# Batch 0's last 64 tokens in 64x64 tiles over two banks, and the last score ahead of the token tail

## The chip, the cores and the metric

The kernel runs on one core of a Trainium2 chip. A core has TensorE (PE, matmuls; PEld is its weight loads), VectorE (DVE), ScalarE (ACT), GpSimd (POOL) and SyncE (SP, which here issues DMAs). They run beside each other and wait for each other through semaphores. TensorE writes its results to PSUM, here eight banks of 128 x 512 fp32, which VectorE and ScalarE read. The metric is the device time of the whole kernel in microseconds (us), as the median of several runs.

## The reference

For 8 batches, 12 heads, 448 tokens and 64 features a head:

```python
scores = q @ k.T / sqrt(64) - log(448)
attn   = sigmoid(scores)                       # no softmax
x      = attn @ v                              # heads side by side: (8, 448, 768)
h      = relu(x.T @ w_tok1) @ w_tok2           # mixes tokens: 448 -> 256 -> 448
u      = x + h.T
out    = u + relu(u @ w_ch1) @ w_ch2           # mixes channels: 768 -> 1536 -> 768
```

The kernel computes in fp16 with fp32 sums.

## The kernel before

Work goes in 24 cycles, three (`u` = 0, 1, 2) to each batch `b`; a cycle handles four heads. All order is written out by hand: each engine runs its instructions in the order in which the program records them, and the framework adds only the waits.

In a cycle, seven calls of `qk` (line 184) make the scores of 64 keys each against all queries: four 64x64 matmuls of 448 columns, one in each quarter of the array, into a two-bank buffer with the tag "qk", of which there are two. ScalarE's sigmoid (line 191) empties the buffer, so score j needs the sigmoid of score j-2. `av` (line 215) sums over the values for the cycle before; `tok_tail` (line 274) and `tok1` (line 293) are the first token matmul of an earlier cycle: the tail has only the last 64 tokens and runs in four 64x64 tiles, the other six matmuls are 128x128; ReLU follows on ScalarE (line 307). `ytrans` (line 316) is the second token matmul.

Between these, output groups of an earlier batch are computed: `ch2` (lines 549, 560 and 572 or 579) for 128 tokens by 384 outputs, and other forms of the same. Batch 0 differs from the later ones: the residual u is not added by VectorE from a transposed copy (`un`), but by three identity matmuls on TensorE, so VectorE only copies (line 579). The last 64 of the 448 tokens are a group of their own. `ch2_last` (lines 802, 813, 825) does it with 24 matmuls in 128x64 tiles (128 contraction rows, 64 tokens), two next to each other for the two halves of the outputs, in one bank; with the residual that is 6 matmuls more. For batches 1 to 6 `last_split` does it in 64x64 tiles instead: the contraction rows 0 to 63 and 64 to 127 go to different banks, `ps[0]` and `ps[1]`, four matmuls in a step (line 631), and VectorE adds the two.

At the end of a batch's third cycle `utrans` and `token_sums` (lines 330 and 442) prepare the next stage, and `sevens` (line 499) does the first channel matmul as seven block products; its first one takes a "qk" buffer.

Besides the two "qk" buffers there are four single banks, m0 to m3; `at_bank` says which is handed out next. Banks 0 and 1 serve the attention and token work, 2 and 3 the channel work.

The cycles c = 6, 7 and 8 (counted from 0; c = 8 has u = 2) spread a list `pending` of batch 0's output pieces over three calls of `work(share)` a cycle. `work` flips between banks 2 and 3 with each group, and after each piece takes one step from `copies` (relayouts of the next batch on VectorE, line 126, and the DMA transposes that follow them). In the cycle c = 8, `work(1)` ends the last full-width group, which is in bank 2; `work(2)` and `work(3)` are the group of the last 64 tokens, in bank 3. From c = 9 a second loop runs to c = 23; here `ch2_pair`, `last_split` and `ch2_split` (lines 375, 631) lie between the scores.

Of the kernel before, what the change touches and what calls it, by code (L numbers as in the profile page):

```python
# [10 lines left out]
FP32 = mybir.dt.float32  # L11
ADD = mybir.AluOpType.add
# [11 lines left out]
NU = 3  # L24
# [6 lines left out]
def kernel(  # L31
# [11 lines left out]
    nc = tc.nc  # L43
# [6 lines left out]
    NCB = CC // 128  # L50
    N_CYCLES = NU * B
    N_FIRST = 4
    DH = D // 2
# [10 lines left out]
    ident = pc.tile([128, 128], FP16, name="ident")  # L64
# [14 lines left out]
    uts = [pc.tile([128, NDB, 512], FP16, name=f"ut{n}") for n in range(2)]  # L79
# [5 lines left out]
    def bank(shape, dtype, name):  # L85

        if opening_banks:
            n = opening_banks.pop(0)
        else:
            n = at_bank[0]  # L90
            at_bank[0] = (n + 1) % 4
        return pp.tile(shape, dtype, tag=f"m{n}", bufs=1, name=name)
# [86 lines left out]
    def qk(b, u, j):  # L179
        att[b, u, j] = pa.tile([128, 2, S], FP16, tag="att", bufs=10, name=f"att_{b}_{u}_{j}")  # L180
        ps = pp.tile([128, 2, 512], FP32, tag="qk", bufs=2, name=f"qk_{b}_{u}_{j}")
        for g in range(2):
            for hi in range(2):
                nc.tensor.matmul(  # L184
                    out=ps[64 * g : 64 * g + 64, hi, 0:S],
                    lhsT=tr[b, "k"][64 * hi : 64 * hi + 64, u, j, 64 * g : 64 * g + 64],
                    rhs=tr[b, "q"][64 * hi : 64 * hi + 64, u, :, 64 * g : 64 * g + 64],
                    start=True,
                    stop=True,
                )  # L190
        nc.scalar.activation(  # L191
            out=att[b, u, j][:, :, :],
            in_=ps[:, :, 0:S],
            func=SIGMOID,
            bias=bias_t[:, :],
            scale=att_scale,
        )
# [427 lines left out]
    def split_steps(ps, n_cb, lhsT, rhs):  # L625

        def step(n):
            for r in range(2):
                part = slice(64 * r, 64 * r + 64)
                for m in (0, 64):  # L630
                    nc.tensor.matmul(  # L631
                        out=ps[r][m : m + 64, 0:DH],
                        lhsT=lhsT(part, n, m),
                        rhs=rhs(part, n, m),
                        start=(n == 0),
                        stop=(n == n_cb - 1),
                    )

        return [lambda n=n: step(n) for n in range(n_cb)]
# [21 lines left out]
    def last_split(b, ps):  # L661

        def end():
            o = pa.tile([128, DH], FP32, tag="outl", bufs=1, name=f"o_{b}_3")
            parts = [slice(0, 64), slice(64, 128)]
            nc.vector.tensor_tensor(
                out=o[:, :].rearrange("s (u d) -> s u d", d=128),
                in0=un[b][:, 0:NU, 3, :],
                in1=ps[0][:, 0:DH].rearrange("s (u d) -> s u d", d=128),
                op=ADD,  # L670
            )
            nc.vector.tensor_tensor(out=o[:, :], in0=o[:, :], in1=ps[1][:, 0:DH], op=ADD)
            for g in range(2):
                nc.sync.dma_start(
                    out=orow[b, NJ - 1][:, DH * g : DH * g + DH], in_=o[parts[g], :]
                )

        return split_steps(
            ps,
            NCB,  # L680
            lambda part, n, m: h2[b][part, BY_GROUP[n], 384:448],
            lambda part, n, m: c2[part, BY_GROUP[n], DH * (m // 64) : DH * (m // 64) + DH],
        ), end

    LOW, HIGH = slice(0, NCB // 2), slice(NCB // 2, NCB)
    D1, D2 = slice(0, DH), slice(DH, D)
# [234 lines left out]
    def pieces_ch2(b, groups):  # L921
        for t, half in groups:
            for n in range(0, NCB, 3):
                yield 3 * DH, lambda t=t, half=half, n=n: ch2(b, t, half, n, n + 3)

    def pieces_last(b):
        for n in range(0, NCB, 3):
            yield 3 * DH, lambda n=n: ch2_last(b, n, n + 3)
# [197 lines left out]
    def some(n):  # L1126
        for f in copies[:n]:
            f()
        del copies[:n]
# [3 lines left out]
    for c in range(2 * NU, ONE_RUN):  # L1133
        b, u = divmod(c, NU)
        before, ahead = divmod(c - 1, NU), divmod(c - 2, NU)


        if c == 2 * NU:
            first = c
            pending, shares = [*pieces_ch2(0, by_half[2:]), *pieces_last(0)], [10, 10, 10]  # L1140
            total = sum(w for w, f in pending)
            spent = 0

        def work(share):
            goal = 3 * sum(shares[: c - first]) + share * shares[c - first]
            done = 0
            while pending and spent + done < total * goal / 90:
                w, f = pending.pop(0)
                if len(pending) % 4 == 3:
                    lane[0] ^= 1  # L1150
                at_bank[0] = 2 + lane[0]
                f()
                done += w
                if copies:
                    copies.pop(0)()
                elif early:
                    early.pop(0)()
            return done

        some(len(copies))  # L1160
        qk(b, u, 0)
        qk(b, u, 1)
        at_bank[0] = 0
        av(*before)
        xtrans_dma(*before)
        qk(b, u, 2)
        if c == 2 * NU + 2:
            copies += through_dma(3, 0)[NU + 1 :]
        spent += work(1)
        qk(b, u, 3)  # L1170
        qk(b, u, 4)
        if u < 2:
            at_bank[0] = 0
            tok_tail(*ahead)
            tok1(*ahead, with_scores=True)
        spent += work(2)
        if c == 2 * NU + 2:
            utrans(b - 1)
            token_sums(b - 1)
            spent += work(3)  # L1180
        qk(b, u, 5)
        qk(b, u, 6)
        at_bank[0] = 0
        if u < 2:
            ytrans(*ahead)
        else:
            tok_tail(*ahead)
            tok1(*ahead, with_scores=True)
        if c == 2 * NU + 1:
            copies += through_dma(3, 0)[: NU + 1]  # L1190
        if u < 2:
            spent += work(3)
        if u == 2:
            sevens(b - 1)
            at_bank[0] = 0
            ytrans(*ahead)
            gated_loads(b)
    assert not copies and not pending and not early

    for c in range(ONE_RUN, N_CYCLES):  # L1200
        b, u = divmod(c, NU)
        before, ahead = divmod(c - 1, NU), divmod(c - 2, NU)
        if b == NU:
            within, behind = ((0, 0), (3, 3), (2, 0))[u]
        else:
            within, behind = ((0, 2), (2, 4), (0, 0))[u] if b < B - 1 else (2, 2)
        if u == 0:
            assert not copies
            copies += through_dma(b + 1, 0) if b + 1 < B else output_sums()

        X, Y = 2, 0
        at_bank[0] = X
        if u == 1:
            ps = [bank([128, 512], FP32, f"c2_{b - 2}_3_{r}") for r in range(2)]
            turn0, last_end = last_split(b - 2, ps)
            qk(b, u, 0)
            qk(b, u, 1)
            for f in turn0:  # L1220
                f()
            last_end()
            qk(b, u, 2)
        else:
            turn0, turn1, rest = ch2_pair(b - 2, u)
            part = len(turn1) * 2 // 3
            qk(b, u, 0)
            qk(b, u, 1)
            for f in turn0:
                f()  # L1230
            qk(b, u, 2)
            some(within)
            if c == ONE_RUN + 2:
                gated_loads(b)
        at_bank[0] = Y
        av(*before, 0, 4)
        qk(b, u, 3)
        av(*before, 4, NJ)
        xtrans_dma(*before)
        if u == 2:  # L1240
            utrans(b - 1)
            token_sums(b - 1)
        qk(b, u, 4)
        if u == 1:
            at_bank[0] = X
            turn1, rest = ch2_split(b - 2, u, 0)
            part = NCB // 2
        for f in turn1[:part]:
            f()
        qk(b, u, 5)  # L1250
        for f in turn1[part:]:
            f()
        if u == 1:
            rest()
            some(within)
        at_bank[0] = Y
        tok_tail(*ahead)
        qk(b, u, 6)
        tok1(*ahead, with_scores=True)
        if u == 1:  # L1260
            at_bank[0] = X
            ch2(b - 2, u, 1)
        else:
            rest()
        if u == 2:
            sevens(b - 1)
        at_bank[0] = Y
        ytrans(*ahead)
        some(behind)
        if u == 1 and NU < b < B - 1:  # L1270
            gated_loads(b)
# [93 lines left out]
```

## Time and profile before

| | |
|---|---|
| median of 3 runs | 344.91 us (344.31 to 345.24) |
| the profiled execution | 343.85 us, of which the span of the instructions is 341.9 |
| granted TensorE clock | 1.000 |
| TensorE busy | 334.7 us (98%) |
| VectorE, ScalarE busy | 216.7 us (63%), 212.5 us (62%) |
| chain that ended last | TensorE 90%, ScalarE 5%, the rest 1% each or less |

In the profile "L184" is line 184 of the kernel. A row of a timeline gives start, length, engine, line, operation, output<-inputs, tile and shape, and how many instructions it holds; in brackets the idle time before it and what ended it. The lengths of matmuls include their way through the array, so matmuls that follow each other overlap in it: what one costs is the time from its start to the next start.

### The profile page before, as it was taken

Reading aid. Unit: us, or ns where it says so; the run is one execution under the profiler, and the core shown is the slowest. Engines: PE = TensorE matmul, PEld = TensorE weight load, DVE = VectorE, ACT = ScalarE, POOL = GpSimd, SP = SyncE. Lnnn points to the kernel's source line nnn. Section 1 sums busy time; section 2 is a strip of 40 time slices with the busy share of each in tenths; the row PEclk is TensorE's granted clock in tenths of the full one; section 3 lists DMA queues with packets and bytes.
Section 4 is the critical chain, followed back from the end, with each engine's and each line's share of the span. In section 5 each row is a group of like instructions: output and inputs, shape, how many; then the busy total and the mean of one; then the engine's idle time right before and its main releaser. Section 6 shows DMA issues by size and latency. Waiting matters only on the chain.

```text
span 341.9 us, 10439 instructions
## 1 busy us (share of the span) xinstructions
PE 334.7 (98%) x4549; PEld 238.8 (70%) x4549; DVE 216.7 (63%) x438; ACT 212.5 (62%) x271; POOL 56.6 (17%) x98
## 2 busy tenths in 40 slices
PE   7999999999999999999999999999999999999994
PEld 4655566555886679766886679766896669768952
DVE  3376467588674775566574584666765685886662
ACT  4996846588658684877648785777648885102400
POOL 8992440040040004000130004000100000000000
PEclk9999999999999999999999999999999999999999
DMA  7999999999999799999999599948991438035406
GB/s 125 172 180 191 207 204 200 169 175 223 219 172 208 119 175 175 209 168 134 191 188 167 123 196 184 223 98 149 199 157 33 102 78 141 5 69 130 86 0 161
DMA packets 104380, 52.17 MB, mean 153 GB/s; under 512 B 76432, under 2 KB 101264, under 8 KB 104336
## 3 DMA queue, kind: packets, MB, share of 16 engines
q1 hardware_dynamic: 78944, 29.70, 47.8%
q0 software_dynamic: 25168, 21.50, 41.7%
q8 instruction: 35, 0.57, 0.7%
q10 hardware_dynamic: 224, 0.33, 0.3%
q14 instruction: 9, 0.07, 0.1%
HBM read 43.45 MB, written 11.01 MB: 159 GB/s over the span
## 4 chain that ended last, share of the span: by engine, by line
PE 90%; ACT 5%; DMA 1%; DVE 1%; issue 1%; ACTq 0%; DVEq 0%
PE c_ab L499 14%; PE qk L184 10%; PE c L549 9%; PE c_c L499 8%; PE c L375 8%; PE xa L215 8%; PE c L631 6%; PE tk L293 5%; PE yt L316 5%; ACT att L191 5%; PE c L763 4%; PE c L613 4%; PE c L352 3%; DMA first_q<-in_q_dram 1%; PE c L802 1%; PE c_a L499 1%
## 5 line engine op out<-in xcount | busy, mean ns | idle before, releaser
L191 ACT ACTIVATE att<-qk,att_bias 128x896 f16<-128x896 f32 x168 | 157.0, 1015 | 41.5 <-PE qk L184 41.1
L184 PE MATMUL qk<-tr_q,tr_k 64*64 64x448 f16 x672 | 57.5, 356 | 0.5 <-DVE tr_k L176 0.2
L499 PEld LDWEIGHTS <-c 128*128 128x128 f16 x504 | 48.4, 98 | 1.1 <-issue 0.3
L224 DVE CAST xT<-xa 128x448 f16<-128x448 f32 x46 | 26.6, 620 | 29.8 <-PE xa L215 29.8
L215 PE MATMUL xa<-att,raw_v 64*64 64x448 f16 x644 | 38.0, 349 | 0.0
L499 PEld LDWEIGHTS <-sum 128*128 128x128 f16 x378 | 36.3, 98 | 0.0
L184 PEld LDWEIGHTS <-tr_k 64*64 64x64 f16 x672 | 20.3, 105 | 19.7 <-issue 12.0
L572 DVE TENSOR_TENSOR o<-un,c 128x384 f32<-128x384 f16 x34 | 18.8, 554 | 23.3 <-PE c L613 10.2
L549 PE MATMUL c<-c,h 128*128 128x384 f16 x180 | 32.9, 326 | 0.0
L375 PE MATMUL c<-c,h 64*64 64x384 f16 x640 | 31.1, 322 | 0.0
L520 ACT ACTIVATE pt_ab<-c_ab 128x896 f32<-128x896 f32 x21 | 19.3, 917 | 16.9 <-PE c_ab L499 16.3
L323 DVE TENSOR_TENSOR ut<-xT,yt 128x448 f16<-128x448 f16 x48 | 27.5, 614 | 1.9 <-PE yt L316 1.9
L215 PEld LDWEIGHTS <-raw_v 64*64 64x64 f16 x672 | 20.3, 107 | 10.9 <-issue 0.4
L1039 POOL COPY gate<-tr_q 128x2 f16<-128x2 f16 x6 | 1.2, 195 | 154.0 <-DMA tr_q<-rel_q 154.0
L549 PEld LDWEIGHTS <-h 128*128 128x128 f16 x180 | 17.2, 98 | 11.3 <-issue 1.0
L307 ACT ACTIVATE h<-tk 128x256 f16<-128x256 f32 x42 | 14.2, 405 | 16.7 <-PE tk L293 16.7
L375 PEld LDWEIGHTS <-h 64*64 64x64 f16 x640 | 18.7, 107 | 7.9
L316 PE MATMUL yt<-w,h 128*128 128x448 f16 x96 | 22.1, 353 | 0.0
L631 PE MATMUL c<-c,h 64*64 64x384 f16 x480 | 22.1, 322 | 0.0
L522 ACT ACTIVATE h<-c_ab 128x896 f16<-128x896 f32 x7 | 6.4, 917 | 24.4 <-PE c_ab L499 24.4
L293 PE MATMUL tk<-xn,w 128*128 128x256 f16 x156 | 21.2, 274 | 0.1
L529 DVE TENSOR_TENSOR h<-pt_ab,c_ab 128x896 f16<-128x896 f32 x14 | 15.2, 1084 | 9.4 <-PE c_ab L499 9.4
(110 smaller groups left out, 473.3 us busy)
## 6 DMA issues: line engine op xcount, KB each, us to landing
out_dram<-o SPq DMA_DIRECT2D x48, 192.0 KB, 3.5
c<-in_moe_w_ch_dram POOLq DMA_DIRECT2D x4, 1152.0 KB, 15.6
raw_k<-in_k_dram POOLq DMA_DIRECT2D x10, 336.0 KB, 9.3
raw_q<-in_q_dram POOLq DMA_DIRECT2D x10, 336.0 KB, 13.3
raw_v<-in_v_dram POOLq DMA_DIRECT2D x10, 336.0 KB, 10.8
out_dram<-o SPq DMA_DIRECT2D x15, 96.0 KB, 2.2
raw_q<-in_q_dram POOLq DMA_DIRECT2D x12, 112.0 KB, 4.9
raw_k<-in_k_dram POOLq DMA_DIRECT2D x12, 112.0 KB, 4.8
```

The source lines that it names most:

```text
L184: nc.tensor.matmul(out=ps[64 * g : 64 * g + 64, hi, 0:S], lhsT=tr[b, "k"][64 * hi : 64 * hi + 64, u, j, 64 * g : 64 * g + 64], rhs=tr[b, " ...
L191: nc.scalar.activation(out=att[b, u, j][:, :, :], in_=ps[:, :, 0:S], func=SIGMOID, bias=bias_t[:, :], scale=att_scale,)
L215: nc.tensor.matmul(out=ps[g][64 * hi : 64 * hi + 64, 0:S], lhsT=raw[b, "v"][64 * g : 64 * g + 64, u, hi, j, :], rhs=att[b, u, j][64 * g : ...
L224: nc.vector.tensor_copy(out=xTs[b % 2][:, u, g, 0:S], in_=ps[g][:, 0:S])
L293: nc.tensor.matmul(out=ps[tcb], lhsT=w1[rows, t, cols], rhs=xn[b, u][rows, :, t, :], start=(t == 0 and not with_scores), stop=(t == (2 if ...
L316: nc.tensor.matmul(out=ps[:, 0:S], lhsT=h1[b, u][:, tcb, g, :], rhs=w2[:, tcb, :, :], start=(tcb == 0), stop=(tcb == 1),)
L323: nc.vector.tensor_tensor(out=uts[b % 2][:, db, 0:S], in0=xTs[b % 2][:, u, g, 0:S], in1=ps[:, 0:S], op=ADD)
L375: nc.tensor.matmul(out=ps[p][m : m + 64, 0:n], lhsT=lhsT(p, part, m), rhs=rhs(p, part), start=(first and turn == 0), stop=(last and turn = ...
L499: nc.tensor.matmul(out=ps[:, g, p, :], lhsT=weights[n][:, d, 128 * cb : 128 * cb + 128], rhs=moving[n][:, d, :], start=(n in (1, 5, 2) and ...
L520: nc.scalar.activation(out=shaped(part[:, :, :]), in_=ps, func=COPYF)
L549: nc.tensor.matmul(out=ps[:, 0:DH], lhsT=h2[b][:, BY_GROUP[cb], 128 * t : 128 * t + 128], rhs=c2[:, BY_GROUP[cb], cols], start=(cb == 0), ...
L631: nc.tensor.matmul(out=ps[r][m : m + 64, 0:DH], lhsT=lhsT(part, n, m), rhs=rhs(part, n, m), start=(n == 0), stop=(n == n_cb - 1),)
```

## The change

It has two parts.

In the cycle c = 8 the last-64-token group of batch 0 leaves `pending` and is done by `last_split`: twelve steps of four 64x64 matmuls and three steps of four 64x64 matmuls with 128 columns for the residual, over banks 2 and 3. `utrans` and `token_sums` are recorded ahead of it, eight steps come before score 5, which stood behind the whole group, and the rest stands between scores 5 and 6. VectorE then copies one bank and adds the other (128x384 each) where it made two copies of 64x384. The goals of `work` stay as they were, since `total` keeps the group's weight.

In the cycles c = 9 to 23, `qk(b, u, 6)` is recorded ahead of `tok_tail` instead of behind it.

```diff
@@ last_split
         def end():
             o = pa.tile([128, DH], FP32, tag="outl", bufs=1, name=f"o_{b}_3")
-            nc.vector.tensor_tensor(
-                out=o[:, :].rearrange("s (u d) -> s u d", d=128),
-                in0=un[b][:, 0:NU, 3, :],
-                in1=ps[0][:, 0:DH].rearrange("s (u d) -> s u d", d=128),
-                op=ADD,
-            )
+            if b in un:
+                nc.vector.tensor_tensor(
+                    out=o[:, :].rearrange("s (u d) -> s u d", d=128),
+                    in0=un[b][:, 0:NU, 3, :],
+                    in1=ps[0][:, 0:DH].rearrange("s (u d) -> s u d", d=128),
+                    op=ADD,
+                )
+            else:
+                nc.vector.tensor_copy(out=o[:, :], in_=ps[0][:, 0:DH])
             nc.vector.tensor_tensor(out=o[:, :], in0=o[:, :], in1=ps[1][:, 0:DH], op=ADD)
...
+        def u_step(n):
+            for r in range(2):
+                part = slice(64 * r, 64 * r + 64)
+                for g in range(2):
+                    nc.tensor.matmul(
+                        out=ps[r][64 * g : 64 * g + 64, 128 * n : 128 * n + 128],
+                        lhsT=uts[b % 2][part, NU * g + n, 384:448],
+                        rhs=ident[part, :],
+                        start=False,
+                        stop=(n == NU - 1),
+                        skip_group_check=True,
+                    )
...
-        ), end
+        ) + [lambda n=n: u_step(n) for n in range(0 if b in un else NU)], end
@@ cycles c = 6, 7, 8
-            pending, shares = [*pieces_ch2(0, by_half[2:]), *pieces_last(0)], [10, 10, 10]
-            total = sum(w for w, f in pending)
+            pending = [*pieces_ch2(0, by_half[2:])]
+            shares = [10, 10, 10]
+            total = sum(w for w, f in pending) + NCB * DH
...
-        spent += work(2)
-        if c == 2 * NU + 2:
+        if u < 2:
+            spent += work(2)
+            qk(b, u, 5)
+        else:
+            assert not pending
+            some(len(copies))
             utrans(b - 1)
             token_sums(b - 1)
-            spent += work(3)
-        qk(b, u, 5)
+            at_bank[0] = 2
+            steps, last_end = last_split(
+                0, [bank([128, 512], FP32, f"c2_0_3_{r}") for r in range(2)]
+            )
+            for f in steps[:8]:
+                f()
+            qk(b, u, 5)
+            for f in steps[8:]:
+                f()
+            last_end()
         qk(b, u, 6)
@@ cycles c = 9 to 23
         at_bank[0] = Y
+        qk(b, u, 6)
         tok_tail(*ahead)
-        qk(b, u, 6)
         tok1(*ahead, with_scores=True)
```

More of the change, by code (lines that the diff above doesn't have):

```diff
@@ L676, in end @@
                 )
+        def u_step(n):
[8 more added lines that the diff above has]
+                        stop=(n == NU - 1),
+                        skip_group_check=True,
+                    )
         return split_steps(
```

## The prediction

> **What bounds the kernel now.** I read the page's busy time and slices first, then the waits of TensorE, then narrow timelines around the two places that the change touches.
>
> ```profile
> PE 334.7 (98%) x4549; PEld 238.8 (70%) x4549; DVE 216.7 (63%) x438; ACT 212.5 (62%) x271; POOL 56.6 (17%) x98
> PE   7999999999999999999999999999999999999994
> PE qk L184 <- DVE tr_k L176: 0.2, 1, 0.2
> PE qk L184 <- ACT att L191: 0.2, 1, 0.2
> ```
>
> TensorE is busy in every slice but the first and last, and the waits view finds under half a microsecond for it after the start. So time is TensorE's order of matmuls: what lengthens or shortens that sequence moves the end one for one; work on the other engines counts only where TensorE comes to wait for it. Short waits hide inside the modelled length of a matmul, so below I take start-to-start times.
>
> The cycle c = 8, TensorE, then VectorE, then ScalarE:
>
> ```profile
> 83.10 0.57 PE L184 MATMUL qk<-tr_q,tr_k 64*64 64x448 f16 x8
> 83.61 2.14 PE L802 MATMUL c<-c,h 128*64 128x384 f16 x24
> 85.58 0.33 PE L813 MATMUL c<-ident,ut 128*64 128x128 f16 x6
> 85.84 0.57 PE L184 MATMUL qk<-tr_q,tr_k 64*64 64x448 f16 x8
> 86.25 0.28 PE L274 MATMUL tk<-xn,w 64*64 64x256 f16 x4
> 86.69 0.60 PE L293 MATMUL tk<-xn,w 128*128 128x256 f16 x4
> 87.40 0.26 PE L499 MATMUL c_ab<-ut,c 128*128 128x224 f16 x1
> ...
> 83.29 0.62 DVE L126 COPY rel_q<-raw_q 128x896 f16<-128x896 f16 x1
> 83.83 0.55 DVE L579 COPY o<-c 128x384 f32<-128x384 f32 x1
> ...
> 86.34 1.01 ACT L191 ACTIVATE att<-qk,att_bias 128x896 f16<-128x896 f32 x1 [0.84 <-PE qk L184]
> ```
>
> Columns are start, length, engine, line. Two things to see. The seventh products' first matmul (L499) starts at 87.40 although the token matmuls before it end their stream at about 87.12: it takes the scores buffer of score 5, whose sigmoid ends at 86.34 + 1.01 = 87.35. And VectorE empties the bank of the last finished output group (L579) only at 83.83 + 0.55 = 84.38, because a relayout copy stands ahead of it.
>
> A later cycle with u = 2, around its last score:
>
> ```profile
> 122.96 1.02 ACT L191 ACTIVATE att<-qk,att_bias 128x896 f16<-128x896 f32 x1
> ...
> 123.97 0.28 PE L274 MATMUL tk<-xn,w 64*64 64x256 f16 x4
> 124.08 0.36 PE L184 MATMUL qk<-tr_q,tr_k 64*64 64x448 f16 x4
> 124.38 0.83 PE L293 MATMUL tk<-xn,w 128*128 128x256 f16 x6
> ```
>
> The sigmoid is score 4's; it frees, at 123.98, the buffer that score 6 takes at 124.08.
>
> **Part one, the cycle c = 8, step by step.** Units first. A quad of four 64x64 matmuls of 384 columns costs 0.1625 us start to start (twelve such quads of line 631 run from 109.04 to the next score at 110.99). A pair of 128x64 tiles costs the same, twelve from 83.61 to 85.58 with one slower start, so the tiling itself saves nothing: 48 matmuls in 12 quads for 24 in 12 pairs. A score is 0.19, a token tail 0.11. A change of tile shape costs 0.10: of the two scores at 83.10 the second starts at 83.32 and streams to 83.50, but line 802 starts at 83.61; and the first group after a change costs 0.02 more (0.21 from the first score to the second, for 0.19).
>
> What goes: two shape changes (into and out of 128x64), 2 x 0.10, and two slow first groups, 0.05. Score 5, moved among the quads, starts its sigmoid about 0.11 earlier while everything behind it shifts later, so the wait of L499 on it, 87.40 against 87.12, goes: 0.28. In all 0.53.
>
> What comes: the two halves of the contraction need two banks at once, 2 and 3. Before, the group used only bank 3, long empty. Bank 2 is the one that line 579 is still emptying: the last full-width group sits there. TensorE is ready for the first quad at 83.50; VectorE is done at 84.38. From the end of an operation to a matmul released by it the trace shows 0.05 (87.35 to 87.40 for ScalarE; the copy of line 254 ends at 31.04 and its reader starts at 31.10 for VectorE). So the first quad starts at 84.43, a stall of 0.93. Score 5 and everything else of TensorE queue behind it; nothing can pass.
>
> Walk: 84.43 + 8 x 0.1625 = 85.73; score 5, 85.92; four quads, 86.57; three quads of 128 columns at 0.055, the spacing of the line 813 pairs, 86.74; score 6, 86.93; tail and shape change 0.21, 87.14; six token matmuls of 0.109, 87.80. Line 499 starts there instead of 87.40: +0.40. The product after it had itself waited 0.02 on a ReLU (88.57 for 88.54), which now has time: +0.38.
>
> The small quads are bounded: 0.055 from the nearest row, or 0.107, the length of a 64x64 weight load, if loads do not overlap; three times 0.05 is +0.15 at most. I take the first, since the 128x64 loads last 0.110 and their pairs still run at 0.055. The Trainium skill ("TensorE: Matmul & The Clock Gate", section "Back-to-back issue gap") gives about 81 ns for a sustained 128-column matmul with its load; by it the sum would be 0.08 higher, an estimate, and lines 813 speak against it here.
>
> VectorE does one copy and one add of 128x384 (0.55 each) for two copies of 64x384 (0.55 each): zero. They still stand behind the token sums, free at about 87.47, and the next reader in that queue, line 529, comes at 89.69 after more than a microsecond of idle time; if that cover were gone they would cost 0.1 at most. The third relayout, its transpose, the un transpose and the two stores keep their order on VectorE and SP.
>
> **Part two, fifteen later cycles.** Score 6 (four loads, four matmuls) goes ahead of the tail (four and four) on TensorE alone; no DMA or other queue changes order. Both are 64x64, and the shape change to the token matmuls costs 0.10 behind a score (124.08 to 124.38, less 0.19) just as behind a tail (86.25 to 86.46, less 0.11). So nothing is saved, and the tail's own operands have long landed. ScalarE cannot use the head start in the cycles with u = 0 and u = 2: its sigmoids run end to end. With u = 1 the sigmoid starts 0.11 sooner, and nobody waits for it.
>
> The cost: score 6 is ready 0.11 earlier, at the tail's old place, and needs score 4's sigmoid. With u = 2: 122.96 + 1.02 + 0.05 = 124.03 against 123.97, a wait of 0.06, and the tail that used to fill it stands behind. Five cycles, +0.30. With u = 0: sigmoid 4 starts at 104.35 and lasts 1.02, so release is at 105.42, and the tail started at 105.42: zero, at worst 0.02. With u = 1 there is over 0.6 of room. A score that had waited at 53.06 was followed after 0.19 by the next 64x64 group, so the wait brings no second cost; the other bound is 0.02 each.
>
> **Sum:** 0.38 + 0.30 = +0.68 us. The profiled execution took 343.85 (span 341.9 and 1.9 around it), so 344.53; the median of the runs shown is 1.06 above that execution, and I forecast 344.91 + 0.68 = 345.6. That is 0.2%, below the 0.3% (1.03 us) that a measurement of this kernel can tell from no change.
>
> **Rivals.**
> *The stall is not paid* (VectorE empties the bank in time, or another bank is given). Then part one saves 0.53 + 0.02 and the sum is -0.25: 344.7. For: the relayout that delays the copy is movable. Against: the changed program keeps it ahead, and its first quad waits for just that copy. 0.07.
> *Waits breed.* Score 6 waits in ten cycles, not five, each with the slow restart (0.06 + 0.02), small quads at 0.107: 0.38 + 0.15 + 0.80 = +1.3, 346.2. For: u = 0 has no slack left, and 0.02 shows after shape changes. Against: 53.06. 0.12.
> *Faster.* ScalarE is the hidden pacer: each score 6 one tail (0.11) sooner lets sigmoid, ReLU and next cycle start sooner, 15 x 0.11 = 1.65 off, less part one: 343.6. It decides if TensorE waits for ScalarE at the cycles' ends. For: with u = 0 line 316 starts only 0.07 after its ReLU. Against: it starts without a gap, and ScalarE idles 41 us for scores. 0.04.
> *The clock drops.* New idle gaps lower TensorE's clock: at 3.60 four warm-up matmuls start 0.21 apart, twice the warm 0.109, and that phase lasted 3 to 5 us; one such stretch costs 1.5 to 2.5: 347.1 to 348.1. Against: 1.13 us of idle before 5.79, then full speed. 0.03. The Trainium skill, in the same page ("HAM oscillation — how this bites in real kernels") asks for idle gaps of over about 3.4 us, which none here would be.
>
> **The numbers.** Forecast 0.74. Medians here scatter by half a microsecond (344.31 to 345.24), so a fifth of it falls above 1.03. Slower: 0.15 + 0.12 + 0.03 = 0.30; faster 0.04; the same 0.59 of the forecast and the 0.07 without a stall, 0.66. The range runs from just below the rival without the stall to just past the breeding one, which leaves out the two outer cases and some scatter: 344.5 to 346.5.
>
> **What would show it.** Right: the first line 631 quad at about 84.43, with TensorE idle some 0.9 before it until line 579; line 499 at 87.80 directly behind the token matmuls; in cycles with u = 2 a gap of 0.22 instead of 0.16 between the last quad and score 6; the first score of c = 9 at 100.72 for 100.34; span 342.6. Wrong: no stall at 83.50, or TensorE's steps of cycles with u = 0 or 1 changed at all.

## The result, and the profile after

The changed kernel takes 345.82 us as the median of 21 runs (344.68 to 349.33), the kernel before 344.93 in as many. The ratio is 1.0037, 95% interval [1.0022, 1.0052], or +1.27 us [0.76, 1.79]: slower, at about the 0.3% that the prediction took as the least that can be told from no change. The plain medians differ by 0.89 us, the lowest times by 0.84 (344.68 and 343.84).

The profiled execution of the changed kernel was one of its longest: 348.23 us, span 346.3. Its page, TensorE and the granted clock, and then its waits of TensorE (us in all, times, longest):

```profile
PE 336.1 (97%) x4579; PEld 239.3 (69%) x4579; DVE 216.9 (63%) x438; ACT 212.8 (61%) x271; POOL 56.9 (16%) x98
PE   6997999999999999999999999999999999999994
PEclk9999899999999999999999999999999999999999
...
PE c L352 <- DMA c<-in_moe_w_ch_dram: 2.0, 1, 2.0
PE tp_q L167 <- DVE raw_q L970: 1.5, 1, 1.5
PE c L631 <- DVE o L579: 0.6, 1, 0.6
```

Two of these have nothing to do with the change: the first loads came late in this execution, TensorE waited 2.0 us for a weight (line 352), and its clock then dropped for one slice. So all that follows compares stages of the traces and not spans. The *first stage* runs from the first score of c = 8 to the first score of c = 9, the *second stage* from there to the first value matmul behind the last cycle. (The expectations below give 194.34 and 194.93 for the second stage, since they end it 0.28 sooner, at the last matmul of line 316; the differences are the same.)

| | first stage | second stage |
|---|---|---|
| before | 20.50 us | 194.62 us |
| changed | 20.76 | 195.21 |

So this execution lost 0.26 + 0.59 = 0.85 us to the change. The cycle c = 8 of the changed kernel, TensorE and then VectorE (everything is 3.5 us later than before, by the late loads; line 686 is the three quads of the residual):

```profile
86.62 0.57 PE L184 MATMUL qk<-tr_q,tr_k 64*64 64x448 f16 x8
87.79 1.49 PE L631 MATMUL c<-c,h 64*64 64x384 f16 x32 [0.60 <-DVE o L579]
89.09 0.39 PE L184 MATMUL qk<-tr_q,tr_k 64*64 64x448 f16 x4
89.28 0.85 PE L631 MATMUL c<-c,h 64*64 64x384 f16 x16
89.93 0.36 PE L686 MATMUL c<-ident,ut 64*64 64x128 f16 x12
90.09 0.39 PE L184 MATMUL qk<-tr_q,tr_k 64*64 64x448 f16 x4
90.28 0.31 PE L274 MATMUL tk<-xn,w 64*64 64x256 f16 x4
90.52 0.83 PE L293 MATMUL tk<-xn,w 128*128 128x256 f16 x6
91.19 0.35 PE L499 MATMUL c_ab<-ut,c 128*128 128x224 f16 x2
...
86.48 0.20 DVE L230 COPY xT<-xT 128x128 f16<-128x128 f16 x1
86.65 0.62 DVE L126 COPY rel_q<-raw_q 128x896 f16<-128x896 f16 x1
87.19 0.55 DVE L579 COPY o<-c 128x384 f32<-128x384 f32 x1
```

The stall is there: the two scores stream until 87.02, the first quad starts at 87.79, 0.05 after the copy of line 579 ends. The row's bracket gives only 0.60, since the scores' modelled lengths cover the rest; start to start it is 0.77. At the other end line 499 follows the token matmuls without a gap (91.19 for 90.52 + 0.66).

The last score in c = 11 (u = 2): ScalarE's sigmoid of score 4, the loads for score 6, and TensorE:

```profile
126.76 1.03 ACT L191 ACTIVATE att<-qk,att_bias 128x896 f16<-128x896 f32 x1
...
127.61 0.11 PEld L184 LDWEIGHTS <-tr_k 64*64 64x64 f16 x1
127.84 0.11 PEld L184 LDWEIGHTS <-tr_k 64*64 64x64 f16 x3
...
127.29 0.66 PE L375 MATMUL c<-c,h 64*64 64x384 f16 x12
127.84 0.38 PE L184 MATMUL qk<-tr_q,tr_k 64*64 64x448 f16 x4
128.03 0.30 PE L274 MATMUL tk<-xn,w 64*64 64x256 f16 x4
128.26 0.50 PE L293 MATMUL tk<-xn,w 128*128 128x256 f16 x3
```

Score 6 starts 0.05 behind the sigmoid's end at 127.79. One of its four weight loads was done ahead, at 127.61; the other three stood behind the waiting matmul and came at 127.84.

The same place in c = 9 (u = 0):

```profile
109.20 0.38 PE L184 MATMUL qk<-tr_q,tr_k 64*64 64x448 f16 x4
109.39 0.30 PE L274 MATMUL tk<-xn,w 64*64 64x256 f16 x4
109.62 0.28 PE L293 MATMUL tk<-xn,w 128*128 128x256 f16 x1
```

From tail to token matmuls it is 0.23 (128.03 to 128.26, and 109.39 to 109.62 with u = 0) where the same step took 0.21 before (86.25 to 86.46); unrounded the difference is 0.03. Cycle by cycle, against before: u = 0 +0.03, u = 1 0.00, u = 2 +0.09, five times each, to the hundredth.

### The profile page after: what moved, and what is told of

It is laid out like the page before. It is cut to its first block, busy times and chain, and to the rows that moved or that the text cites. A ratio compares the mean times of both kernels' runs of the same rounds, so it can differ in the third digit from the quotient of the medians.

```text
span 346.3 us, 10499 instructions
## 1 busy us (share of the span) xinstructions
PE 336.1 (97%) x4579; PEld 239.3 (69%) x4579; DVE 216.9 (63%) x438; ACT 212.8 (61%) x271; POOL 56.9 (16%) x98
## 4 chain that ended last, share of the span: by engine, by line
PE 86%; DMA 5%; POOL 4%; ACT 2%; issue 1%; DVE 1%; DVEq 0%; ACTq 0%; POOLq 0%
PE c_ab L499 14%; PE qk L184 9%; PE c L549 8%; PE c_c L499 8%; PE c L375 8%; PE xa L215 7%; PE c L631 6%; PE yt L316 5%; PE tk L293 5%; PE c L780 4%; PE c L613 4%; DMA c<-in_moe_w_ch_dram 4%; PE c L352 3%; ACT att L191 2%; DMA w2s<-in_moe_w_tok_dram 2%; PE c_b L499 1%
## 5 line engine op out<-in xcount | busy, mean ns | idle before, releaser
L184 PE MATMUL qk<-tr_q,tr_k 64*64 64x448 f16 x672 | 58.2, 359 | 0.5 <-ACT att L191 0.2
L184 PEld LDWEIGHTS <-tr_k 64*64 64x64 f16 x672 | 21.1, 105 | 20.7 <-issue 12.1
L375 PE MATMUL c<-c,h 64*64 64x384 f16 x640 | 31.1, 322 | 0.0
L631 PE MATMUL c<-c,h 64*64 64x384 f16 x528 | 24.4, 323 | 0.6 <-DVE o L579 0.6
L375 PEld LDWEIGHTS <-h 64*64 64x64 f16 x640 | 18.7, 107 | 7.9
L631 PEld LDWEIGHTS <-h 64*64 64x64 f16 x576 | 17.1, 107 | 7.8 <-issue 0.9
```

What stands on the lines that cost most here:

```text
L184: nc.tensor.matmul(out=ps[64 * g : 64 * g + 64, hi, 0:S], lhsT=tr[b, "k"][64 * hi : 64 * hi + 64, u, j, 64 * g : 64 * g + 64], rhs=tr[b, " ...
L375: nc.tensor.matmul(out=ps[p][m : m + 64, 0:n], lhsT=lhsT(p, part, m), rhs=rhs(p, part), start=(first and turn == 0), stop=(last and turn = ...
L631: nc.tensor.matmul(out=ps[r][m : m + 64, 0:DH], lhsT=lhsT(part, n, m), rhs=rhs(part, n, m), start=(n == 0), stop=(n == n_cb - 1), skip_gro ...
```

## The experiments

Part one and part two by themselves, and two ways to take the stall away, ran on one chip.

**Part one alone** (the later cycles as before):

```diff
-        qk(b, u, 6)
         tok_tail(*ahead)
+        qk(b, u, 6)
         tok1(*ahead, with_scores=True)
```

> Part one alone: the group of the last 64 tokens in 64x64 tiles in c = 8; the later cycles as before. Measured in the profile from the first score of c = 8 to the first score of c = 9 (20.50 us before, 20.76 after) and from there to the first value matmul behind the last cycle (194.34 before, 194.93 after). Theory (the bank wait): first stage +0.26, second stage 0.00, whole kernel +0.3 us. Rival (the later swap is free, as both orders cost TensorE the same, and what is lost lies in part one alone): the whole +0.9 appears here.

The second stage was 194.62, as before: the later cycles are indeed unharmed. But the first stage of this execution was 23.90, 3.4 longer than before, which neither theory had foreseen. Median 345.29 against 344.99 us, ratio 1.0020 [0.9996, 1.0045]. So the theory's +0.26 cannot be read from this execution. Its waits, VectorE's timeline and a table by windows (mean granted clock behind the busy times):

```profile
PE c L631 <- DVE o L579: 2.1, 1, 2.1
...
84.40 0.20 DVE L230 COPY xT<-xT 128x128 f16<-128x128 f16 x1
86.09 0.62 DVE L126 COPY rel_q<-raw_q 128x896 f16<-128x896 f16 x1 [1.50 <-DMA raw_q<-in_q_dram]
86.63 0.55 DVE L579 COPY o<-c 128x384 f32<-128x384 f32 x1
...
88.00:90.00 2.00, 2.00 (x36) 1.54 (x31) 1.93 (x6) 0.52 (x1) 0.00 (x0) 0.58 1.28 291
```

The relayout that stands ahead of line 579 waits for batch 3's query load. In this execution the load landed 1.5 us late; line 579, and with it bank 2 and TensorE, waited along. Behind that gap of 2.1 us the granted clock was 0.50 for one stretch of 3.4 us. In the kernel before bank 2 is not asked for at this time, so the same wait should stay on VectorE; the runs with a late load below test this.

**Part two alone** (the kernel before, with score 6 ahead of the tail).

> Part two alone: score 6 ahead of the token tail in c = 9 to 23, the cycle c = 8 as before. Theory (score 6 runs into score 4's sigmoid and its quarters start apart): first stage 0.00, second stage +0.59, that is 0.03 in each cycle with u = 0, 0.09 with u = 2 and nothing with u = 1; whole kernel +0.6 us. Rival (the swap is free): both stages unchanged.

First stage 20.50, second 195.21: +0.59 and nothing else, as the theory has it. (This theory was written after the changed kernel's trace had shown the 0.59; what is new is that part two brings it alone.) Median 345.43 against 344.99 us, ratio 1.0010 [0.9985, 1.0035]; by times alone this could not be told from no change.

**Line 579 first.** Part one alone, and in c = 8 no relayout is taken within `work`:

```diff
-                if copies:
+                if copies and c < 2 * NU + 2:
                     copies.pop(0)()
-                elif early:
+                elif early and not copies:
                     early.pop(0)()
```

> Part one alone, and VectorE empties bank 2 (line 579) ahead of the relayout that stood before it; the three relayouts follow together. Theory (bank wait): the copy starts 0.54 sooner, the stall shrinks from 0.77 to about 0.25 and the first stage is 0.28 shorter than before (20.22). Rival (64x64 quads with the score between them cost more than the pairs, whatever the bank does): first stage stays at +0.26 (20.76).

First stage 20.30, 0.20 shorter than before, where 0.28 was expected: the copy started 0.46 sooner and not 0.54, and the first quad still waited 0.32. The sign is the theory's: quads are not dearer than pairs. Median 345.26 against 344.99 us, ratio 1.0009 [0.9983, 1.0036], not told apart.

**Other banks.** Part one alone, with the group in banks 3 and 0; what follows takes its banks in a matching order.

```diff
-    def sevens(b, banks=(2, 3, 0, 1, 0)):
+    def sevens(b, banks=(0, 1, 2, 3, 2)):
...
-            at_bank[0] = 2
+            at_bank[0] = 3
             steps, last_end = last_split(
...
+            at_bank[0] = 1
             tok_tail(*ahead)
...
-            sevens(b - 1)
-            at_bank[0] = 0
+            sevens(b - 1, (1, 0, 3, 2, 3))
+            at_bank[0] = 2
...
-        X, Y = 2, 0
+        X, Y = 0, 2
```

> Part one alone, with the group in banks 3 and 0, which are empty by then, instead of 2 and 3; the token tail of c = 8 takes 1 and 2, and everything behind has the two pairs of banks exchanged. Theory (bank wait): no stall at the first quad, the two shape changes and the wait of line 499 stay saved, first stage 0.50 shorter than before (20.00), second stage unchanged, whole kernel -0.5 us, which beats both kernels. Rival (quads cost more): first stage +0.26.

First stage 19.97, so 0.54 shorter than before, second stage 194.62; median 344.73 against 344.99 us, ratio 0.9982 [0.9963, 1.0001]. Without the stall the quads follow the scores at once, with no wait of TensorE on line 579 left:

```profile
84.41 0.57 PE L184 MATMUL qk<-tr_q,tr_k 64*64 64x448 f16 x8
84.82 1.47 PE L631 MATMUL c<-c,h 64*64 64x384 f16 x32
...
87.31 0.28 PE L274 MATMUL tk<-xn,w 64*64 64x256 f16 x4
87.52 0.83 PE L293 MATMUL tk<-xn,w 128*128 128x256 f16 x6
```

Where the medians cannot tell these four kernels from the one before, the lowest times agree with the stages (+0.26 for part one by the changed kernel's trace, then +0.59, -0.20 and -0.54): +0.25 us for part one, +0.52 for part two, -0.22 with line 579 first and -0.54 with other banks (12 runs each, against 35 of the kernel before).

Three smaller claims follow, each from one profiled execution.

**Part two where there is room**: score 6 ahead of the tail only for u = 1.

> Part two in the cycles with u = 1 alone (five of fifteen). Theory: score 6 has 0.6 us of room there, so the order of score and tail is free: every cycle as long as before (8.30, 10.25 and 20.38 us). Rival (the order itself costs, as a shape change behind a tail is dearer than behind a score): +0.03 to +0.09 in these cycles too.

Every cycle as before (8.30, 10.25, 20.38 us). The order itself is free.

**Score 6 earlier still.**

```diff
-        for f in turn1[part:]:
+        for f in turn1[part:-1]:
             f()
+        qk(b, u, 6)
+        turn1[-1]()
...
-        qk(b, u, 6)
         tok_tail(*ahead)
```

> Part two alone, with score 6 one quad (0.16 us) earlier still, in c = 9 to 23. Theory (it waits for score 4's sigmoid to the nanosecond, and the quarters that start apart cost 0.03 at the next change of shape): u = 0 +0.19 over before, u = 2 +0.25, u = 1 0.00 (it has over 0.5 us of room); 15 cycles +2.2 us. Rival (the wait is absorbed by the next group, as TensorE's stream is only shifted): as with part two, +0.03 and +0.09, +0.6 in all.

u = 0 +0.19, u = 1 0.00, u = 2 +0.25; the second stage +2.18. That is the 0.03 and 0.09 of part two and the whole quad of 0.16 on top: the time by which score 6 is ready too soon is waited out, and nothing takes it in.

**Score 5 behind the group again.** Part one, with `qk(b, u, 5)` behind `last_end()`.

> Part one alone with score 5 behind the whole group again, as before. Theory: line 499 waits once more for score 5's sigmoid, so with the quads' start taken as it falls, the time from the group's last matmul to line 499 is back at 1.6 us (1.26 with score 5 among the quads, less its own 0.19 there), 0.28 of it a gap ahead of line 499. Rival (the gap ahead of line 499 came of the 128x64 shape): no gap there.

The gap ahead of line 499 is back: the six token matmuls end their stream at 88.88 + 0.66 = 89.54, and line 499 starts 0.28 later. The first stage is 21.05, 0.29 longer than with score 5 among the quads.

```profile
88.88 0.83 PE L293 MATMUL tk<-xn,w 128*128 128x256 f16 x6
89.82 0.35 PE L499 MATMUL c_ab<-ut,c 128*128 128x224 f16 x2
```

**A late load on purpose.** The long first stage of part one asked for this: the same delay in three kernels, on one chip. (The copies turned out to last longer than the 2.2 and 3.7 us that the expectations give: twelve took 3.15 to 4.00 us in the three profiles, and twenty, in a fourth run, 6.04.)

```diff
+        if b == 1:
+            for _ in range(12):
+                nc.gpsimd.tensor_copy(
+                    out=gate[:, :], in_=tr[b + 1, "q"][:, NU - 1, NJ - 1, 126:128]
+                )
         if b + 2 < B:
             load(b + 2, "q", q, 0, NU)
```

With part one:

> Part one alone, and batch 3's query load is issued about 2.2 us later (twelve tiny GpSimd copies ahead of it). Theory (line 579, which frees bank 2, stands on VectorE behind a relayout that waits for this load, so a late load reaches TensorE): the first quad starts some 2 us later than in the changed kernel, at 6 to 7 us after the first score of c = 8 instead of 4.4, and the first stage is 22.5 us or more instead of 20.76; where TensorE's gap exceeds 2 us the granted clock halves for one stretch of 3.4 us, and the stage is 24. Rival (the load's time does not matter; the long first stage seen with part one alone came of the clock): stage at 20.8.

Median 351.28 against 345.26 us, ratio 1.0150 [1.0075, 1.0226]. In the profile the load ended VectorE's wait 5.85 us late, more than the delay put in, and TensorE stood 6.46 us and ran at half clock behind it:

```profile
90.26 0.62 DVE L126 COPY rel_q<-raw_q 128x896 f16<-128x896 f16 x1 [5.85 <-DMA raw_q<-in_q_dram]
91.40 2.77 PE L631 MATMUL c<-c,h 64*64 64x384 f16 x32 [6.46 <-DVE o L579]
...
91.00:95.00 4.00, 3.60 (x48) 2.54 (x51) 3.38 (x8) 0.34 (x1) 0.00 (x0) 0.50 1.06 225
```

The first stage was 28.65. The rival falls: the clock adds to it, but the load's lateness starts it.

With the kernel before:

> The kernel before with the same late load. Theory: the group of the last 64 tokens uses bank 3, so VectorE's wait stays off TensorE's path; first stage 20.5 as without the delay, at most 0.5 more if the token sums come too late for the seventh products. Rival (a late load costs TensorE in any order): first stage longer by the same 2 us as with part one.

Median 347.18 against 345.26 us, ratio 1.0024 [0.9983, 1.0066], so the same delay costs far less than with part one. It need not be free, since the plain medians differ by 1.9 us. The profile does not show what the delay does to the stage: the whole beginning of that execution ran late, the load was in time after all, and the stage was 20.50.

With part one in banks 3 and 0:

> Part one in banks 3 and 0 with the same late load. Theory: the quads start on time (3.67 us after the first score of c = 8); the late load shows only where VectorE's queue frees a bank for line 499 after the token sums, so the first stage is between 20.0 and 21.5, well under that of part one in banks 2 and 3. Rival: as long as part one's.

Median 347.72 against 345.26 us, ratio 1.0067 [1.0029, 1.0106]. The quads started on time (3.67), but the stage was 21.94, over the upper end expected: line 499's second product waited 1.4 us for VectorE's copy of line 675, which stands behind the relayouts and the token sums.

```profile
89.97 1.31 PE L499 MATMUL c_ab<-ut,c 128*128 128x224 f16 x12
92.65 0.73 PE L499 MATMUL c_a<-ut,c 128*128 128x224 f16 x6 [1.36 <-DVE o L675]
```

In this execution VectorE waited 2.15 us for the load (85.80 to 87.94), against 5.85 in part one's profile, so the two stages cannot be set side by side. Of the 2.15 us 1.97 reached TensorE (21.94 for 19.97): the bank order of this version is open to a late load too, though the median of its runs is 3.6 us below part one's.

**The kernel before with a later load**, to see in a trace what its order does with one:

> The kernel before with batch 3's query load issued about 3.7 us later (twenty tiny GpSimd copies). With L the time from the end of VectorE's line 230 copy to its first query relayout, which waits for the load: theory, first stage 20.50 + max(0, L - 3), since VectorE's delay reaches TensorE only through the token sums that the seventh products need from 9.9 us on; with part one the same load costs its whole L (e8_late_part1: L 5.85, stage 28.6). Rival (a late load costs any order the same): 20.5 + L.

```profile
83.00 0.19 DVE L230 COPY xT<-xT 128x128 f16<-128x128 f16 x1
86.97 0.62 DVE L126 COPY rel_q<-raw_q 128x896 f16<-128x896 f16 x1 [3.78 <-DMA raw_q<-in_q_dram]
...
90.67 2.47 PE L499 MATMUL c_ab<-diffs,sum 128*128 128x224 f16 x24 [0.17 <-DVE diffs L442]
```

L was 3.78 and the first stage 20.85: 3.4 of the 3.78 us cost nothing in this stage, and the rest came through the token sums, as the theory has it (its allowance of 3 was a little small). Profiles without an added delay agree: with score 6 ahead of the tail only for u = 1, and with score 6 earlier still, VectorE waited 0.9 and 0.5 us for this load, and the first stage was 20.50 all the same. What the theory had left out: c = 10 took 1.24 us more, where line 274 waited 1.0 us for its transposed input.

**The better version.** As the other banks above, and the products that follow take the banks that the ReLUs free:

```diff
-            n = at_bank[0]
+            n = at_bank[0] % 4
...
-    def sevens(b, banks=(0, 1, 2, 3, 2)):
+    def sevens(b, banks=(3, 0, 1, 2, 1)):
...
-            sevens(b - 1, (1, 0, 3, 2, 3))
-            at_bank[0] = 2
+            sevens(b - 1, (3, 0, 1, 2, 1))
+            at_bank[0] = 1
...
-        X, Y = 0, 2
+        X, Y = 3, 1
```

> The candidate for a better version: part one in banks 3 and 0 as in e4_banks, but the seventh products that follow at once take banks 1 and 2, which the ReLUs free, so that none of them stands behind VectorE's token sums; later cycles with all four banks turned by one. No part two. Theory: first stage 19.97 us (before 20.50), second stage 194.62 as before, whole kernel -0.5 us or 0.9985 of before. Rival (the gain of e4_banks was chance): first stage 20.5.

First stage 19.97, second 194.62, median 344.56 against 345.06 us, ratio 0.9986 [0.9964, 1.0007]. Both versions with free banks gain the same 0.54 us in their traces; their ratios come to 0.62 and 0.48 us, their plain medians to 0.26 and 0.50, and each interval by itself still holds 1. That the second one stands a late load better was not tried.

## Why the prediction was right or wrong

The median, 345.8, lies 0.2 from the forecast of 345.6 and within the range. The ratio, 1.0037, lies a little outside the likeliest class, within 0.3%, with an interval that reaches to both sides; the plain medians (0.89 us) and the trace (0.85) lie inside it. That the sum came so near is in part luck: part one cost 0.26 where 0.38 was forecast and part two 0.59 where 0.30 was, and the two errors have opposite signs.

*The stall at bank 2* was right in place and cause: line 631 waits for line 579. It was 0.77 for 0.93: in the execution before, VectorE's relayout had itself waited some 0.15 us for its load, which I read as a fixed cost. The step that failed here is that one, the copy's end taken from one execution as if nothing in front of it could vary. What stood ahead of it was a DMA, and in the profile of part one it came 1.5 us late, in the delayed one 5.85. Of the ten profiled executions without an added delay, four show VectorE waiting for this load, by 0.1, 0.5, 0.9 and 1.5 us.

*What goes* (0.53) was right: without the stall the stage is 0.54 shorter, and the 0.28 at line 499 comes back alone when score 5 goes back. The small quads cost 0.055 each (89.93 to 90.09 for three), as the nearest row said.

*Part two* was right in its place (u = 2 by the sigmoid, u = 1 free) and mis-sized: +0.59 for +0.30. One of the prediction's own signs of being wrong appeared, a change in the cycles with u = 0. The sentence that failed is "so the wait brings no second cost". The other bound, 0.02 a wait, was the true one, at 0.03, in ten cycles: with u = 0 the release falls on the very time at which score 6 is ready, and that is enough. I had looked at the start behind a score that had waited at 53.06. There the next group was 64x64 too, and one quarter of the array simply ran ahead of the other three by 0.03; the price falls due at the next change of tile shape, which then comes 0.03 later, as if it waited for the last quarter. The trace had it: behind scores that had waited (at 42.80 and 54.86), shape changes took 0.13 instead of 0.10.

```profile
42.80 0.38 PE L184 MATMUL qk<-tr_q,tr_k 64*64 64x448 f16 x4 [0.15 <-ACT att L191]
43.12 0.36 PE L352 MATMUL c<-ut,c 128*128 128x448 f16 x1
```

Part one pays the same: behind its stalled quad the step from tail to token matmuls took 0.24 (90.28 to 90.52), and with other banks, where nothing waits, 0.21 (87.31 to 87.52). The rival in which waits breed had this mechanism, with too high a price for the waits with u = 0 (0.08 each for 0.03) and for the small quads.

*The rest.* The trace accounts for 0.85 us, the ratio for 1.27 [0.76, 1.79]. The interval holds the trace's value, and the medians and the lowest times, 0.89 and 0.84 apart, lie by it, so no further cost is shown. Executions whose query load comes late would lie higher, since part one now hands that lateness to TensorE; that it does so is shown, how often it does in the plain changed kernel is not. *The clock* did drop, behind part one's long waits, at idle gaps that the prediction held to be too short; the 0.77 us of the changed kernel's profile did not lower it.

## What to carry to other kernels

When work moves into a buffer, price the wait by what stands on the queue ahead of the instruction that frees it, and ask whether a load is among it: an engine that had slack may hand a DMA's lateness to the one that has none. A wait of nearly nothing in packed small tiles is not free: here it put the tiles 0.03 us out of step, which was paid at the next shape change. And a reordering that is free where the awaited engine has time to spare (here u = 1) costs where that engine works without a break and its result is needed sooner (u = 0 and u = 2).

## What was not expected of the hardware

A gap of 2.1 us in TensorE's work was followed by a granted clock of 0.50 for 3.4 us (part one alone), and the gap of 2.0 us at line 352 in the changed kernel's profile likewise by 3.4 us of 0.50; gaps of 1.4 us (part one in banks 3 and 0 with a late load) did not show it. A gap of 1.8 us at line 352 (the kernel before with a late load) was followed by 3.4 us of it as well, and the one of 6.46 us by 6.8. In the three shorter cases the lower clock began only 0.3 to 1.1 us after the work had resumed. The Trainium skill ("TensorE: Matmul & The Clock Gate", section "What's actually happening") ties the return to half clock to an idle window of about 3.4 us: the stretch's length agrees, but here shorter gaps were enough.

Of four matmuls that go to the four quarters of the array, only the first one's weights were loaded while it waited for its buffer (one load at 127.61, three at 127.84), and the quarters stayed 0.03 us apart until the tile shape changed.
